# Stage 1 of the first batch in a written order: loads pinned ahead of the projection weights, and products of a zeroed tile at the start

## The chip, the cores and the metric

The kernel runs on one core of a Trainium2 chip. The metric is the device time of the whole program in microseconds (us), as the median of several runs. The engines are TensorE (PE; PEld is its weight load), VectorE (DVE), ScalarE (ACT), GpSimd (POOL) and SyncE (SP), whose queue issues every DMA of this kernel.

## The reference, cut to what matters

Three blocks follow each other, for 2 batches of 768 positions:

- a local attention (8 heads of 64): every position attends to the keys less than 16 away and to 24 block keys, which are the maxima of the keys over blocks of 32; its values are the 48 or 96 values around it and 24 block means. `a = exp(s - max); a / (sum + 1e-9)`, then `a @ v_all`. This is stage 1.
- a layer of 4 experts, each a causal attention (`x @ wq`, `x @ wk`, `x @ wv`, softmax, `a @ v @ wo`), two of them kept for each position by the gate.
- a mixer: `relu(xt @ w_tok1) @ w_tok2` added over the positions, and `relu(u @ w_ch1) @ w_ch2` over the channels, whose weights come as 64-bit floats and are decoded on the chip.

## The kernel before

Stage 1 of one batch works on 4 pairs of heads (hp), each in 3 groups (g) of 4 tiles of 64 queries: 12 groups, numbered 0 to 11. A group goes through these steps:

- `s1_scores` (L205): 4 float32 products of 128x120 into one PSUM bank. One float32 product is two passes in the trace, so a group has 8 rows.
- the minima with the mask (L214, DVE), the exponentials with their sums (L217, ACT), `1e-9` added (L222, POOL), the reciprocal (L223, DVE), the normalization (L225, POOL, one instruction for batch 0);
- `s1_turn` (L233): 4 transposes, copied out by ACT (L235);
- `s1_values` (L244): 8 products (16 passes), copied to x0h by ACT (L248), and the rest of the rounding to x0l by DVE (L249).

Once for a pair of heads, `s1_keys` writes the block maxima into the key tile kx (for the first pair, L170 to L180 also build kx from one plain key tile kt), and `s1_means` makes the block means of batch 0 with 12 products (24 passes, L193), copies them out (ACT, L198) and spreads them into the value tile vx (POOL, L199). Batch 1 sums its means on DVE instead (L186, from the tile vt).

The loads of batch 0 (L156) are kx or kt, the two halves of the queries qb, and vx for each pair; the masks and the identity come with the first. The weights of the projections are loaded by `w_load` (L536, L540: rv and rqk) and split into a high and a low part by `split_w` (L112 on POOL, L113 on DVE, the last quarter on POOL): wv first, then wqk.

The order of the instructions on each engine is found by the framework, which plays the program through with its own costs. What the program text sets is only the order in which `run` draws from its generators. Pinned to the order of the text were the loads of the first two pairs of heads alone (`tc.keep_in_program_order`). `tc.issue_after(x)` puts what a block holds behind `x` on the engine of `x`, with no wait across engines.

Stage 1 of batch 1 and the projections of batch 0 (`proj`: pv, then pj) are drawn together after stage 1 of batch 0. Then come the attention of the experts of batch 0, the projections of batch 1, and the decoding of the mixer's weights (`decode_w`), which stands behind the last x1h on ACT (`gate`).

Of the kernel before, what the change touches and what calls it, by code (L numbers as in the profile page):

```python
# [7 lines left out]
F32 = mybir.dt.float32  # L8
F32R = mybir.dt.float32r
AF = mybir.ActivationFunctionType  # L10
ALU = mybir.AluOpType
# [22 lines left out]
BK = {"sc": 3, "pt": 3, "acc": 2}  # L34
NEGB = -8.0e9
BIG = 3.0e38

F64_TINY = 2.0 ** -15
F64_HUGE = 122880.0
# [3 lines left out]
def stack_kernel(ctx: ExitStack, tc, qT, kT, kwT, vw, vT, wqkv, wo, tok1, tok2, ch1, ch2,  # L43
# [64 lines left out]
        nc.sync.dma_start(raw, src)  # L108
        return raw

    def split_w(hi, lo, r, sub=None):
        gps.tensor_scalar(hi, r, 1.0, 1.0, op0=ALU.mult, op1=ALU.mult)  # L112
        (sub or vec).tensor_sub(lo, r, hi.bitcast(F32))  # L113

    def decode_w(hi, lo, src, n):

# [22 lines left out]
    def s1_load(b, hp, qb):  # L139
        first = b == 0 and hp == 0  # L140
        kx = unit([P, NT, KX], F32, f"kx{b}{hp}")
        kt = None
        if first:

            kt = xunit([P, S + 2 * WIN], F32, "kt")
            vec.memset(kx[:, 0, KW:KX], 0.0)

        vt = half([P, S], F32, "vt") if b else None
        vx = unit([P, NT, P], F32, f"vx{b}{hp}")
        loads = [(kt, kT) if first else (kx, kwT[b, hp])]  # L150
        loads += [(qb[i::2, :, i, :], qT[b, hp, i::2].rearrange("p (t c) -> p t c", c=P)) for i in range(2)]
        if first:
            loads += [(lmask, lmask_d), (ident, ident_d), (blocks, blocks_d)]
        loads += ([(vt, vT[b, hp])] if b else []) + [(vx[:KW], vw[b, hp])]
        for d, src in loads:
            r = nc.sync.dma_start(d, src)  # L156
            if b == 0 and hp < 2:
                tc.keep_in_program_order(r)
        last["load"] = r
        return kt, vt, kx, vx  # L160

# [18 lines left out]
                vec.tensor_copy(*sums)  # L180

    def s1_sums(kt, vt, kx, vx):
        if vt is None:
            return None
        vs = sp1.tile([P, NBLK], F32, name="vs")
        vec.tensor_reduce(vs, vt.rearrange("p (n c) -> p n c", c=BLK), axis=AX.X, op=ALU.add)  # L186
        return vs

    def s1_means(b, hp, vs, vx):
        pv = bank("pt", f"vm{b}{hp}")  # L190
        if vs is None:
            for t in range(NT):
                ten.matmul(pv[:NBLK, :P], blocks[:, 2 * (NT - 1 - t):2 * (NT - 1 - t) + NBLK], vx[:KW, t, :],  # L193
                           start=t == 0, stop=t == NT - 1)
        else:
            ten.transpose(pv[:NBLK, :P], vs, ident)
        vm = sp1.tile([NBLK, P], F32, name="vm")
        act.activation(vm, pv[:NBLK, :P], AF.Copy, scale=1.0 if vs is None else 1.0 / BLK)  # L198
        gps.tensor_scalar(vx[KW:KX], vm[:, None, :].broadcast_to([NBLK, NT, P]), 1.0, 1.0, op0=ALU.mult, op1=ALU.mult)  # L199

    def s1_scores(b, hp, g, qb, kx):
        sc = bank("sc", f"s1s{b}{hp}{g}")
        for i in range(4):
            t = 4 * g + i
            ten.matmul(sc[:, KX * i:KX * i + KX], qb[:, t // 2].rearrange("p i c -> p (i c)")[:, t % 2::2], kx[:, t, :],  # L205
                       start=True, stop=True)
        n = sp1.tile([P, 4, KX], F32, name="n", bufs=2)
        mn = sp1.tile([P, 4], F32, name="mn", bufs=4)
        sm = sp1.tile([P, 4], F32, name="sm", bufs=4)
        pr = sp1.tile([P, 4, KX], F32, name="pr", bufs=3)  # L210
        for i in range(4):
            t = 4 * g + i
            mi = 0 if t == 0 else (2 if t == NT - 1 else 1)
            vec.tensor_tensor_reduce(n[:, i, :], sc[:, KX * i:KX * i + KX], lmask[:, mi, :],  # L214
                                     scale=-0.125, scalar=BIG, op0=ALU.add, op1=ALU.min, accum_out=mn[:, i:i + 1])
        for i in range(4):
# [3 lines left out]
    def s1_norm(b, pr, sm):  # L220
        ri = sp1.tile([P, 4], F32, name="ri", bufs=4)
        gps.tensor_scalar(sm, sm, 1e-9, 1.0, op0=ALU.add, op1=ALU.mult)  # L222
        vec.reciprocal(ri, sm)  # L223
        if b == 0:
            gps.tensor_mul(pr, pr, ri[:, :, None].broadcast_to([P, 4, KX]))  # L225
# [4 lines left out]
    def s1_turn(b, hp, g, pr, sm):  # L230
        pT = bank("pt", f"s1p{b}{hp}{g}")
        for i in range(4):
            ten.transpose(pT[:KX, P * i:P * i + P], pr[:, i, :], ident)  # L233
        pTs = sp1.tile([P, 512], F32, name="pTs", bufs=2)
        act.activation(pTs[:KX], pT[:KX], AF.Copy)  # L235
        return pTs

    def s1_values(b, hp, g, vx, pTs, xh, xl):
# [7 lines left out]
        cs = slice(256 * g, 256 * g + 256)  # L246
        hi, lo = xh[hp // 2][:, hp % 2, cs], xl[hp // 2][:, hp % 2, cs]
        last["x"] = act.activation(hi, av[:, :256], AF.Copy)  # L248
        return lambda: vec.tensor_sub(lo, av[:, :256], hi.bitcast(F32))  # L249

    def s1(b, xh, xl, qbs, lds):

        n = 3 * HP
        nq = len(qbs)
        if lds is None:
            lds = [s1_load(b, 0, qbs[0])]
        st, tr, rest = {}, {}, {}
        s1_keys(*lds[0])
        for i in range(n + 4):
            hp, g = divmod(i, 3)  # L260
            if i < n:
                st[i] = s1_scores(b, hp, g, qbs[hp % nq], lds[hp][2])
                if g == 0 and len(lds) < min(hp + 2, HP):
                    lds.append(s1_load(b, hp + 1, qbs[(hp + 1) % nq]))
            if 0 <= i - 1 < n:
                s1_norm(b, *st[i - 1])
            if i < n:
                if g == 0:
                    vs = s1_sums(*lds[hp])
                if g == 1:  # L270
                    s1_means(b, hp, vs, lds[hp][3])
                    if hp + 1 < HP:
                        s1_keys(*lds[hp + 1])
            if 0 <= i - 2 < n:
                tr[i - 2] = s1_turn(b, *divmod(i - 2, 3), *st[i - 2])
            if i - 4 in rest:
                rest[i - 4]()
            if 0 <= i - 3 < n:
                hp, g = divmod(i - 3, 3)
                rest[i - 3] = s1_values(b, hp, g, lds[hp][3], tr[i - 3], xh, xl)  # L280
            if i < n:
                yield

# [248 lines left out]
    raws = [xunit([P, HP, 260], F32, "rv"), *(xunit([P, HP, 2, P], F32, f"rqk{p}") for p in range(2))]  # L532

    def w_load(i):
        if i == 0:
            nc.sync.dma_start(raws[0], wsrc[:, :, 512:772])  # L536
        else:
            for t in range(2):
                c = 256 * t + P * (i - 1)
                nc.sync.dma_start(raws[i][:, :, t], wsrc[:, :, c:c + P])  # L540
# [20 lines left out]
    g1 = s1(1, *xs[1], qbs[:2], None)  # L561
# [8 lines left out]
    def wt_load():  # L570
        for nm, src, kt_n, n, step in (("t1", tok1, 6, 256, 256), ("t2", tok2, 2, 768, 256), ("wo", wo, 2, 512, 512)):
# [102 lines left out]
```

## Time and profile before

| | us |
|---|---|
| median of 3 runs | 470.71 (470.41 to 471.19) |
| profiled execution, whole time | 472.78 |
| its span, first to last instruction | 470.9 |
| its mean granted clock | 0.992 |
| bytes moved | 46.51 MB |

The page gives the busy share of each engine over the whole span, the span in 40 slices, the chain of work that ended last, and the costliest groups of instructions. A timeline lists instructions in order of time, merged where they follow each other, with the idle time before them in brackets and what ended it. [...]

### The profile page before, as it was taken

How to read it: one execution, taken by the hardware profiler on the slowest of the kernel's cores; microseconds unless marked ns; L12 is line 12 of the kernel's file. 1: busy time of each engine (PE TensorE's matmuls, PEld its weight loads, DVE VectorE, ACT ScalarE, POOL GpSimd, SP SyncE). 2: the span in 40 equal slices, each digit the busy share in tenths (PEclk: the TensorE clock that was granted, in tenths of full speed). 3: DMA queues.
4: the chain of work that ended last, by engine and by line, in shares of the span. 5: the costliest groups of instructions: out<-in, count | busy, mean ns of one | idle time of the engine just before them, and what ended most of it. 6: DMA issues, size and time to landing. Idle time of an engine off the chain costs nothing.

```text
span 470.9 us, 8508 instructions
## 1 busy us (share of the span) xinstructions
PE 445.4 (95%) x3012; PEld 420.4 (89%) x3012; DVE 281.8 (60%) x817; ACT 230.3 (49%) x653; POOL 286.0 (61%) x319
## 2 busy tenths in 40 slices
PE   3998999999989969999999999999999999999996
PEld 3886999889978757888799999999999999999996
DVE  6666665749699759777864643676572673322322
ACT  2666865877778766875764333224324231110110
POOL 5674732758989877898783879877864772000000
PEclk9999999999999997999999999999999999999999
DMA  8999527706515873120211111121221110001111
GB/s 265 289 306 308 150 57 215 170 2 157 134 46 156 202 183 86 46 90 1 89 47 46 45 47 45 46 89 46 89 85 50 47 45 1 0 1 67 68 68 68
DMA packets 28522, 46.51 MB, mean 99 GB/s; under 512 B 2496, under 2 KB 19648, under 8 KB 28480
## 3 DMA queue, kind: packets, MB, share of 16 engines
q1 hardware_dynamic: 28480, 45.97, 34.7%
q8 instruction: 24, 0.39, 0.4%
q14 instruction: 18, 0.15, 0.1%
HBM read 33.38 MB, written 3.15 MB: 78 GB/s over the span
## 4 chain that ended last, share of the span: by engine, by line
PE 70%; DMA 10%; DVE 9%; POOL 5%; issue 3%; ACT 2%; SPq 0%; DVEq 0%; ACTq 0%; POOLq 0%
PE h L102 7%; PE h L103 7%; PE h L101 7%; PE o L101 7%; PE o L102 7%; PE o L103 7%; DMA kx<-in_kwT_dram 5%; PE s1s L205 3%; PE s1a L244 2%; PE u L101 2%; DMA vx<-in_vw_dram 2%; PE u L102 2%; PE u L103 2%; PE s2s L371 2%; PE s2p L397 2%
## 5 line engine op out<-in xcount | busy, mean ns | idle before, releaser
L127 POOL TENSOR_SCALAR deca<-deca 128x512 f32<-128x512 f32 x30 | 57.9, 1934 | 13.4 <-ACT deca L126 12.6
L102 PE MATMUL o<-hl,c2h 128*128 128x384 f32 x192 | 64.2, 337 | 0.0
L103 PE MATMUL o<-hh,c2l 128*128 128x384 f32 x192 | 64.0, 336 | 0.0
L97 ACT ACTIVATE hh<-h 128x384 fp32r<-128x384 f32 x48 | 23.2, 488 | 78.7 <-PE h L103 76.6
L98 DVE SCALAR_TENSOR_TENSOR hl<-h,hh 128x384 fp32r<-128x384 f32 x48 | 26.5, 555 | 53.3 <-ACT hh L97 53.3
L500 DVE TENSOR_TENSOR oa<-o,oa 128x384 f32<-128x384 f32 x64 | 31.9, 549 | 38.3 <-PE o L103 38.3
L101 PE MATMUL o<-hh,c2h 128*128 128x384 f32 x192 | 49.4, 336 | 0.0
L217 ACT ACTIVATE pr<-n,mn 128x120 f32<-128x120 f32 x96 | 36.6, 384 | 22.2 <-DVE mn L214 21.8
L133 POOL TENSOR_TENSOR raw<-raw 128x512 f32<-128x512 f32 x30 | 31.3, 1044 | 21.1 <-DVE raw L130 19.3
L387 POOL TENSOR_SCALAR pr<-pr,f,wg 128x128 f32<-128x128 f32 (+5 forms) x48 | 40.2, 850 | 4.9 <-DVE f L384 1.7
L134 POOL TENSOR_TENSOR deca<-deca,raw 128x512 f32<-128x512 f32 x30 | 40.8, 1359 | 1.0
L132 ACT ACTIVATE raw<-raw 128x512 f32<-128x512 uint32 x30 | 20.3, 677 | 36.5 <-DMA raw<-in_ch_dram 31.5
L128 DVE TENSOR_SCALAR deca<-deca 128x512 int32<-128x512 int32 x30 | 27.5, 918 | 15.2 <-POOL deca L127 15.2
L381 ACT ACTIVATE pr<-pr,mn 128x128 f32<-128x128 f32 (+5 forms) x48 | 32.1, 669 | 9.2 <-DVE mn L376 9.2
L102 PEld LDWEIGHTS o<-hl,c2h 128*128 128x128 f32 x192 | 36.0, 188 | 0.4 <-DVE hl L98 0.3
L103 PEld LDWEIGHTS o<-hh,c2l 128*128 128x128 f32 x192 | 36.0, 188 | 0.0
L205 PE MATMUL s1s<-kx,qb 128*128 128x120 f32 x192 | 28.6, 300 | 7.7 <-DVE wvl L113 7.7
L101 PEld LDWEIGHTS o<-hh,c2h 128*128 128x128 f32 x192 | 34.8, 188 | 0.1
L205 PEld LDWEIGHTS s1s<-kx,qb 128*128 128x128 f32 x192 | 26.6, 212 | 8.2 <-DVE wvl L113 7.7
L102 PE MATMUL h<-u0l,c1h 128*128 128x384 f32 x96 | 32.5, 338 | 0.0
L101 PE MATMUL h<-u0h,c1h 128*128 128x384 f32 x96 | 32.5, 338 | 0.0
L103 PE MATMUL h<-u0h,c1l 128*128 128x384 f32 x96 | 32.3, 337 | 0.0
(202 smaller groups left out, 1327.3 us busy)
## 6 DMA issues: line engine op xcount, KB each, us to landing
raw<-in_ch_dram SPq DMA_DIRECT2D x24, 512.0 KB, 3.6
kx<-in_kwT_dram SPq DMA_DIRECT2D x7, 720.0 KB, 10.2
vx<-in_vw_dram SPq DMA_DIRECT2D x8, 576.0 KB, 9.4
qb<-in_qT_dram SPq DMA_DIRECT2D x16, 192.0 KB, 8.4
raw<-in_tok_dram SPq DMA_DIRECT2D x6, 512.0 KB, 4.5
out_dram<-oa SPq DMA_DIRECT2D x16, 192.0 KB, 2.0
vt<-in_vT_dram SPq DMA_DIRECT2D x4, 384.0 KB, 10.1
rqk<-in_wqkv_dram SPq DMA_DIRECT2D x4, 256.0 KB, 10.3
```

The source lines that it names most:

```text
L101: ten.matmul(out, lh, rh, start=start, stop=False)
L102: ten.matmul(out, lh, rl, start=False, stop=False)
L103: ten.matmul(out, ll, rh, start=False, stop=stop)
L127: gps.tensor_scalar(af, af, F64_TINY, F64_HUGE, op0=ALU.max, op1=ALU.min)
L128: vec.tensor_scalar(ta, ta, 3, 0x3FFFFFFF, op0=ALU.logical_shift_left, op1=ALU.bitwise_and)
L133: gps.tensor_mul(lf, lf, ef)
L134: gps.tensor_add(af, af, lf)
L205: ten.matmul(sc[:, KX * i:KX * i + KX], qb[:, t // 2].rearrange("p i c -> p (i c)")[:, t % 2::2], kx[:, t, :], start=True, stop=True)
L217: act.activation(pr[:, i, :], n[:, i, :], AF.Exp, bias=mn[:, i:i + 1], scale=-1.0, accum_out=sm[:, i:i + 1])
L381: act.activation(prs[r], prs[r], AF.Exp, bias=mn[:, r, ci:ci + 1], scale=-1.0, accum_out=sm[:, r:r + 1])
L387: gps.tensor_scalar(prs[r][:, :nk], prs[r][:, :nk], f[:, r:r + 1], wg[:, 3 * h + r, e:e + 1], op0=ALU.mult, op1=ALU.mult)
L500: vec.tensor_add(oa[d], a[:, :HALF], oa[d])
```

## The change

The steps of stage 1 of batch 0 are taken apart into functions of their own (`s1_minima`, `s1_exps`, `s1_sm`, `s1_ri`, `s1_mul`, `s1_turned`, `s1_high`, `s1_low`), which compute what they did. A new function calls them in the order of a written list, and each instruction that a word of the list traces is tied behind the one traced last on its engine. In the list a word is a step and a group (or a pair of heads): S scores, mn minima, ex exponentials, sm, ri, mu normalization, T transposes, pT their copy, V values, xh and xl the outputs, kx keys, vm a third of the means' products, vme their copy, vx their spreading, wh and wl the split of wv. The words km do nothing. Instructions that are not in the list (the projections, batch 1) may still be placed between them.

```diff
+FIRST = """
+kx0 S0 S1 mn0 ex0 S2 mn1 vm0.0 ex1 sm0 mn2 vm0.1 ri0 km1 mu0 vm0.2 ex2 kx1 sm1 T0 ri1 S3 mu1 pT0 S4
+vme0 sm2 mn3 vx0 ex3 T1 ri2 mn4 S5 mu2 pT1 V0 mn5 ex4 sm3 vm1.0 ri3 km2 mu3 V1 xh0 T2 kx2 sm4 xh1 T3
+xl0 ex5 vm1.1 ri4 xl1 mu4 vm1.2 pT2 sm5 S6 ri5 pT3 mu5 vme1 S7 mn6 vx1 ex6 T4 mn7 T5 S8 km3 ex7 sm6
+V2 ri6 kx3 mu6 V3 mn8 xh2 S9 sm7 pT4 xl2 xh3 ri7 S10 pT5 mu7 mn9 ex8 T6 xl3 T7 V4 ex9 sm8 mn10 V5
+wh0 S11 ri8 wh1 wl0 wh2 pT6 vm2.0 wl1 sm9 wh3 xh4 wl2 mu8 pT7 vm2.1 xl4 ex10 ri9 wl3 vm2.2 mn11 mu9
+T8 vme2 vm3.0 xh5 vx2 ex11 xl5 vm3.1 vm3.2 sm10 ri10 sm11 mu10 ri11 V6 vme3 V7 vx3 pT8 T9 xh6 T10
+xh7 xl6 pT9 mu11 xl7 V8 V9 xh8 pT10 T11 xl8 xh9 V10 pT11 xl9 V11 xh10 xl10 xh11 xl11
+"""
...
         for d, src in loads:
-            r = nc.sync.dma_start(d, src)
-            if b == 0 and hp < 2:
-                tc.keep_in_program_order(r)
+            if b == 0:
+                r = tc.keep_in_program_order(nc.sync.dma_start(d, src))
+            else:
+                with tc.issue_after(last["load"].ins):
+                    r = nc.sync.dma_start(d, src)
         last["load"] = r
...
+    def s1_first(xh, xl, qbs, lds, wsplit):
...
+        for word in FIRST.split():
+            at = len(traced)
+            op = word.rstrip("0123456789.")
+            if op == "vm":
+                block(*map(int, word[2:].split(".")))
+            elif op != "km":
+                step(op, int(word[len(op):]))
+            prev = {}
+            for x in traced[:at]:
+                prev[x.engine] = x
+            for x in traced[at:]:
+                if x.engine in prev:
+                    tc.add_manual_dep(x, prev[x.engine].name, NOSYNC, reason="keep_in_program_order")
+                prev[x.engine] = x
...
+        with tc.issue_after(last["mn", 0, HP - 1, 2].ins):
+            s1_keys(*lds[0])
...
-                if g == 0:
-                    vs = s1_sums(*lds[hp])
-                if g == 1:
-                    s1_means(b, hp, vs, lds[hp][3])
-                    if hp + 1 < HP:
-                        s1_keys(*lds[hp + 1])
+                with tc.issue_after(last["mn", b, hp, 0].ins):
+                    vs = s1_sums(*lds[hp])
+                s1_means(b, hp, vs, lds[hp][3])
+                if hp + 1 < HP:
+                    s1_keys(*lds[hp + 1])
...
+    idle = dec.tile([P, P], F32, tag="raw", name="idle")
+    vec.memset(idle, 0.0)
+    spare = bank("acc", "spare")
+    for i in range(13):
+        tc.keep_in_program_order(ten.matmul(spare[:, :P], idle, idle, start=True, stop=True))
...
     def w_split():
-        for w, r in zip((wv, *wqk), raws):
+        for w, r in zip(wqk, raws[1:]):
             for k in range(HP):
-                split_w(w[0][:, k], w[1][:, k], r[:, k], gps if k == HP - 1 else vec)
+                with tc.issue_after(last["mul"].ins):
+                    split_h(w[0][:, k], r[:, k])
+                    with tc.issue_after(last["mn", 0, HP - 1, 2].ins):
+                        split_l(w[0][:, k], w[1][:, k], r[:, k], gps if k == HP - 1 else vec)
                 yield
...
         lds.append(s1_load(0, hp, qbs[hp]))
-        for i in ((), (0, 1), (2,), ())[hp]:
-            w_load(i)
-    with tc.issue_after(last["load"].ins):
-        nc.sync.dma_start(tri, tri_d)
-        nc.sync.dma_start(cmask, cmask_d)
+    for i in range(3):
+        w_load(i)
+    for t, src in ((tri, tri_d), (cmask, cmask_d)):
+        last["load"] = tc.keep_in_program_order(nc.sync.dma_start(t, src))
+    head = last["load"]
...
-    run((12, s1(0, *xs[0], qbs, lds)), (3 * HP, w_split(), 0.3, 1))
+    s1_first(*xs[0], qbs, lds, [
...
-    run((12, g1), (18, part(p0, 10)))
+    run((12, g1), (18, part(p0, 10)), (2 * HP, w_split(), 0, 0.3))
...
-                    with tc.issue_after(gate.ins):
+                    with tc.issue_after(gate.ins), tc.issue_after(head.ins):
```

`w_load` pins its loads as well. So the SP queue begins with all loads of batch 0, then rv, the four rqk, tri and cmask; the loads of batch 1 and of the mixer's weights follow. The buffer of kt is taken one place earlier among the units it shares with rv and rqk.

## Rows read from the trace of the kernel before

**Rows 1.** The page, part 1: busy time, share of the span, instructions of each engine.
```profile
PE 445.4 (95%) x3012; PEld 420.4 (89%) x3012; DVE 281.8 (60%) x817; ACT 230.3 (49%) x653; POOL 286.0 (61%) x319
```

**Rows 2.** Windows: busy time of each engine, clock, DMA share, GB/s.
```profile
5.00:10.00 5.00, 2.27 (x11) 2.31 (x11) 3.67 (x11) 0.00 (x0) 2.65 (x5) 1.00 1.11 301
10.00:15.00 5.00, 5.00 (x35) 4.77 (x35) 3.75 (x28) 4.18 (x21) 1.38 (x3) 1.00 1.07 307
47.00:105.00 58.00, 57.98 (x599) 53.30 (x598) 34.70 (x195) 42.41 (x172) 30.88 (x73) 1.00 0.48 121
120.00:200.00 80.00, 70.95 (x427) 61.59 (x426) 63.47 (x189) 59.88 (x156) 68.29 (x70) 0.96 0.47 119
```

**Rows 3.** Timeline of PE: start, us, instruction, count, idle before and its releaser.
```profile
7.73 5.22 PE L205 MATMUL s1s<-kx,qb 128*128 128x120 f32 x24 [7.73 <-DVE wvl L113]
12.87 2.80 PE L193 MATMUL vm<-vx,blocks 96*24 96x128 f32 x24
...
33.72 0.65 PE L233 MATMUL s1p<-ident,pr 128*120 128x128 f32 x4 [0.24 <-POOL pr L225]
...
37.80 0.54 PE L233 MATMUL s1p<-ident,pr 128*120 128x128 f32 x3 [0.59 <-POOL pr L225]
...
41.57 0.69 PE L244 MATMUL s1a<-pTs,vx 120*64 120x64 f32 x16 [0.93 <-ACT pr L217]
...
45.09 0.69 PE L244 MATMUL s1a<-pTs,vx 120*64 120x64 f32 x16 [0.84 <-DVE ri L223]
```

**Rows 4.** The chain that ended last, 0 to 130: start, us, what.
```profile
2.25 4.71 DMA qb<-in_qT_dram
...
16.80 11.49 DMA kx<-in_kwT_dram
...
46.68 0.44 PE s1p L233 x4
47.11 0.94 PE s1s L205 x8
...
49.97 0.61 PE s1a L244 x16
```

**Rows 5.** Windows to 45.71 of L205, L193, L233 and L244, in this order.
```profile
0.00:45.71 45.71, 14.24 (x91) 13.30 (x91) 1.00 1.02 290
...
0.00:45.71 45.71, 11.57 (x96) 9.40 (x96) 1.00 1.02 290
...
0.00:45.71 45.71, 5.98 (x36) 3.86 (x36) 1.00 1.02 290
...
0.00:45.71 45.71, 5.85 (x128) 4.60 (x128) 1.00 1.02 290
```

**Rows 6.** Timelines of DVE and POOL: start, first keys, first normalization.
```profile
0.95 1.51 DVE L524 MEMSET qb<- 128x768 f32 x2 [0.95 <-PEq L663]
...
3.72 0.95 DVE L170 TENSOR_REDUCE km<-kt 128x24 f32<-128x768 f32 x1 [1.23 <-DMA kt<-in_kT_dram]
...
6.00 0.51 DVE L180 COPY kx<-km 128x288 f32<-128x288 f32 x1
...
12.58 0.99 POOL L225 TENSOR_TENSOR pr<-pr,ri 128x480 f32<-128x480 f32 x1 [0.55 <-DVE ri L223]
```

**Rows 7.** Groups by line, 7.7 to 47: count, busy us, mean ns, idle before.
```profile
L217 ACT ACTIVATE pr<-n,mn 128x120 f32<-128x120 f32 x44 | 16.8, 382 | 18.6 <-DVE mn L214 18.5
...
L113 DVE TENSOR_TENSOR wqk0l<-rqk,wqk0h 128x256 fp32r<-128x256 f32 x3 | 2.0, 694 | 1.6 <-POOL wqk0h L112 1.6
...
L112 POOL TENSOR_SCALAR wqk0h<-rqk 128x256 fp32r<-128x256 f32 x4 | 1.8, 460 | 1.5 <-DMA rqk<-in_wqkv_dram 1.4
```

**Rows 8.** Timeline of POOL: the first decoding instruction.
```profile
104.36 3.82 POOL L127 TENSOR_SCALAR deca<-deca 128x512 f32<-128x512 f32 x2 [4.27 <-ACT deca L126]
```

**Rows 9.** Waits of the SP queue, and its issue of batch 1's last keys.
```profile
SPq L344 <- ACT s000h L93: 16.8, 1, 16.8
...
74.88 0.77 SPq L156 DMA_DIRECT2D kx<-in_kwT_dram  x1
```

More of the change, by code (lines that the diff above doesn't have):

```diff
@@ L190, in s1_means @@
         pv = bank("pt", f"vm{b}{hp}")
[L191 to L196, printed above, removed]
+        ten.transpose(pv[:NBLK, :P], vs, ident)
         vm = sp1.tile([NBLK, P], F32, name="vm")
-        act.activation(vm, pv[:NBLK, :P], AF.Copy, scale=1.0 if vs is None else 1.0 / BLK)
+        act.activation(vm, pv[:NBLK, :P], AF.Copy, scale=1.0 / BLK)
         gps.tensor_scalar(vx[KW:KX], vm[:, None, :].broadcast_to([NBLK, NT, P]), 1.0, 1.0, op0=ALU.mult, op1=ALU.mult)
@@ L206, in s1_scores, with s1_minima, s1_exps @@
                        start=True, stop=True)
+        return sc
+    def s1_minima(b, hp, g, sc):
         n = sp1.tile([P, 4, KX], F32, name="n", bufs=2)
         mn = sp1.tile([P, 4], F32, name="mn", bufs=4)
+        for i in range(4):
+            t = 4 * g + i
+            mi = 0 if t == 0 else (2 if t == NT - 1 else 1)
+            last["mn", b, hp, g] = vec.tensor_tensor_reduce(
+                n[:, i, :], sc[:, KX * i:KX * i + KX], lmask[:, mi, :],
+                scale=-0.125, scalar=BIG, op0=ALU.add, op1=ALU.min, accum_out=mn[:, i:i + 1])
+        return n, mn
+    def s1_exps(n, mn):
         sm = sp1.tile([P, 4], F32, name="sm", bufs=4)
@@ L211, in s1_scores, with s1_sm, s1_ri, s1_mul @@
         for i in range(4):
[L212 to L216, printed above, removed]
             act.activation(pr[:, i, :], n[:, i, :], AF.Exp, bias=mn[:, i:i + 1], scale=-1.0, accum_out=sm[:, i:i + 1])
         return pr, sm
-    def s1_norm(b, pr, sm):
+    def s1_sm(sm):
+        gps.tensor_scalar(sm, sm, 1e-9, 1.0, op0=ALU.add, op1=ALU.mult)
+    def s1_ri(sm):
         ri = sp1.tile([P, 4], F32, name="ri", bufs=4)
-        gps.tensor_scalar(sm, sm, 1e-9, 1.0, op0=ALU.add, op1=ALU.mult)
         vec.reciprocal(ri, sm)
+        return ri
+    def s1_mul(b, pr, ri):
         if b == 0:
-            gps.tensor_mul(pr, pr, ri[:, :, None].broadcast_to([P, 4, KX]))
+            last["mul"] = gps.tensor_mul(pr, pr, ri[:, :, None].broadcast_to([P, 4, KX]))
         else:
@@ L233, in s1_turn, with s1_turned @@
             ten.transpose(pT[:KX, P * i:P * i + P], pr[:, i, :], ident)
+        return pT
+    def s1_turned(pT):
         pTs = sp1.tile([P, 512], F32, name="pTs", bufs=2)
@@ L245, in s1_values, with s1_out, s1_high @@
                            pTs[:KX, P * i + 64 * j:P * i + 64 * j + 64], start=True, stop=True)
[L246 to L251, printed above, removed]
+        return av
+    def s1_out(hp, g, x):
+        return x[hp // 2][:, hp % 2, 256 * g:256 * g + 256]
+    def s1_high(hp, g, av, xh):
+        last["x"] = act.activation(s1_out(hp, g, xh), av[:, :256], AF.Copy)
@@ new lines, in s1_low, with block, mean, step @@
+    def s1_low(hp, g, av, xh, xl):
+        vec.tensor_sub(s1_out(hp, g, xl), av[:, :256], s1_out(hp, g, xh).bitcast(F32))
+    def s1_first(xh, xl, qbs, lds, wsplit):
+        box = {}
+        def block(hp, p):
+            if p == 0:
+                box["vm", hp] = bank("pt", f"vm0{hp}")
+            pv, vx = box["vm", hp], lds[hp][3]
+            for t in range(4 * p, 4 * p + 4):
+                ten.matmul(pv[:NBLK, :P], blocks[:, 2 * (NT - 1 - t):2 * (NT - 1 - t) + NBLK], vx[:KW, t, :],
+                           start=t == 0, stop=t == NT - 1)
+        def mean(hp):
+            box["vme", hp] = sp1.tile([NBLK, P], F32, name="vm")
+            act.activation(box["vme", hp], box["vm", hp][:NBLK, :P], AF.Copy)
+        def step(op, i):
+            hp, g = divmod(i, 3)
+            if op == "S":
+                box["S", i] = s1_scores(0, hp, g, qbs[hp], lds[hp][2])
+            elif op == "mn":
+                box["mn", i] = s1_minima(0, hp, g, box["S", i])
+            elif op == "ex":
+                box["ex", i] = s1_exps(*box["mn", i])
+            elif op == "sm":
+                s1_sm(box["ex", i][1])
+            elif op == "ri":
+                box["ri", i] = s1_ri(box["ex", i][1])
+            elif op == "mu":
+                s1_mul(0, box["ex", i][0], box["ri", i])
+            elif op == "T":
+                box["T", i] = s1_turn(0, hp, g, box["ex", i][0])
+            elif op == "pT":
+                box["pT", i] = s1_turned(box["T", i])
+            elif op == "V":
+                box["V", i] = s1_values(0, hp, g, lds[hp][3], box["pT", i])
+            elif op == "xh":
+                s1_high(hp, g, box["V", i], xh)
+            elif op == "xl":
+                s1_low(hp, g, box["V", i], xh, xl)
+            elif op == "kx":
+                s1_keys(*lds[i])
+            elif op == "vme":
+                mean(i)
+            elif op == "vx":
+                gps.tensor_scalar(lds[i][3][KW:KX], box["vme", i][:, None, :].broadcast_to([NBLK, NT, P]), 1.0, 1.0,
+                                  op0=ALU.mult, op1=ALU.mult)
+            elif op == "wh":
+                wsplit[i][0]()
+            elif op == "wl":
+                wsplit[i][1]()
+        traced = nc.cur_bb.bb.instructions
+        for word in FIRST.split():
[12 more added lines that the diff above has]
+                prev[x.engine] = x
@@ L253, in s1 @@
+    def s1(xh, xl, qbs):
+        b = 1
         n = 3 * HP
         nq = len(qbs)
[L255 to L258, printed above, removed]
+        lds = [s1_load(b, 0, qbs[0])]
+        ex, pTs, av = {}, {}, {}
+        with tc.issue_after(last["mn", 0, HP - 1, 2].ins):
+            s1_keys(*lds[0])
         for i in range(n + 4):
@@ L530, in stack_kernel @@
     wsrc = wqkv.rearrange("(k p) n -> p k n", p=P)
-    raws = [xunit([P, HP, 260], F32, "rv"), *(xunit([P, HP, 2, P], F32, f"rqk{p}") for p in range(2))]
+    raws = [xunit([P, HP, 260], F32, "rv"), xunit([P, HP, 2, P], F32, "rqk0")]
+    kt0 = xunit([P, S + 2 * WIN], F32, "kt")
+    raws.append(xunit([P, HP, 2, P], F32, "rqk1"))
     def w_load(i):
         if i == 0:
-            nc.sync.dma_start(raws[0], wsrc[:, :, 512:772])
+            tc.keep_in_program_order(nc.sync.dma_start(raws[0], wsrc[:, :, 512:772]))
         else:
```

41 lines of the change are left out of this document (25 added, 16 removed).

## The prediction

> **What bounds the kernel now.** I read the page's engine shares first: TensorE is busy 95% of the span [rows 1], so time can be gained where it stands still or works slowly, and only if the engines behind it follow. Then the windows [rows 2]. From 47 to 105 us TensorE is busy 57.98 of 58.00 us while no other engine reaches 43: there the end moves with the amount of TensorE work still to be done. From 120 to 200 us it is busy 70.95 of 80.00, with POOL at 68.29 and DVE at 63.47. The waste that this change can reach lies before 47 us. The PE timeline [rows 3] shows it as three things: nothing runs until 7.73; the first 24 passes of scores take from 7.73 to 12.87, 0.214 us each, where eight of the same passes take 0.94 us, 0.1175 each, once the stage runs [rows 4]; and between 33 and 45 us there are waits of 0.24, 0.59, 0.93 and 0.84 us for the softmax of this stage.
>
> [...]
>
> **The sum, step by step.** The work of stage 1 of batch 0 on TensorE at full pace, by passes: 96 of scores at 0.1175 (0.94/8), 48 transposes at 0.11 (0.44/4), 192 of values at 0.038 (0.61/16) [rows 4], 96 of means at 0.117 (2.80/24) [rows 3]: 11.3 + 5.3 + 7.3 + 11.2 = 35.1 us.
>
> Before: by 45.71 the trace has 91, 36, 128 and 96 of these [rows 5], worth 10.7 + 4.0 + 4.9 + 11.2 = 30.8 us, in the 37.98 us since 7.73. So 7.2 us were lost: 5.14 - 24 x 0.1175 = 2.3 to the slow pace, 2.6 to the four waits, and the remaining 2.3 to small gaps at changes from one kind of product to another. What is missing is worth 35.1 - 30.8 = 4.3 us. Had TensorE done only this work, it would have ended at 50.0.
>
> After, the start. The zeroed tile needs one DVE instruction at its start, which before was at 0.95 us [rows 6]; a memset six times as large took 0.75 us, so TensorE can begin at about 1.3. 13 float32 products of 128 columns are 26 passes; no row shows one, so I scale the slow scores' pass by 128/120: 0.228 us, 5.9 us for all. They end at about 7.2 if all are slow, and at about 6.6 if the last five run at full pace, as scores did after 5.1 us of work. S0 waits for nothing longer: the keys of the first pair were built by 6.51 [rows 6], and the queries, which landed at 6.96 with rv and one rqk ahead of them [rows 4], now have only kt ahead. I take 6.9 for the start of S0, at full pace.
>
> [...]
>
> After, the written order. I followed each engine through the list with the durations of the trace. T0 has to wait for mn0, ex0, sm0, ri0 and mu0; before, that took from 9.43 (S0's end) to 13.57 [rows 6], 4.1 us. The list puts S1, S2 and vm0 there, 2 x 0.94 + 2.8 = 4.7 us of TensorE. Later each T has at least five TensorE words between it and its scores. ACT has the next largest load, an exponential of a tile every 0.38 us [rows 7], 18.3 us for 48, under 31 with its copies, against 35.1 of TensorE. With in-order engines I find no wait of TensorE over 0.2 us. The pinned order has a price: a late load stands in front of everything behind it on DVE (kx1 before ri1, kx3 before mn8). By the shapes in the code kt is 400 KiB, the queries of a pair 384, the masks 261, vx 576, kx 720. kt landed at 3.7 [rows 6], and from there on some 300 GB/s flowed, 293 KiB/us [rows 2]. Before, that puts the fourth pair's kx, the 7,245th KiB with rv and rqk ahead, at 3.7 + 6,845/293 = 27.1; it landed at 28.3 [rows 4], 1.2 late. In the new order kx1 is the 2,341st KiB, at 10.3, or 11.5 if as late, needed at 11 to 12; kx3 the 5,701st, at 21.8 to 23, needed at 24.5. So 0 to 1 us is lost there, and I take 0.3. The small gaps need not vanish: at the rate of before they are 2.6 us; the list puts longer runs of one kind together, so I take half, 1.3 (0 to 2.6).
>
> Together: 6.9 + 35.1 + 0.3 + 1.3 = 43.6 against 50.0, a gain of 6.4 us. At best 6.6 + 35.1 = 41.7, a gain of 8.3. At worst 7.2 + 35.1 + 1 + 2.6 + 2.3 (scores slow again) = 48.2, a gain of 1.8.
>
> **What is moved.** The loads of rv, rqk, tri and cmask, some 1.8 MiB or 6 us of DMA, fall behind the other loads of batch 0. rv, the 7,181st KiB, lands at about 27 and is first needed at wh0, behind mu7, at about 28; rqk lands at about 30. SP's queue otherwise issues the same loads, and batch 1's first pair (2,064 KiB more) lands by 38 to 40, before TensorE asks for it at 43: nothing. Without this cover the first projection would wait up to 3 us. The splits of wqk fall behind mu11 on POOL and mn11 on DVE: 8 x 0.46 + 2 x about 0.7 = 5.1 us of POOL and 6 x 0.69 = 4.2 of DVE [rows 7], issued from about 40 us on instead of from 17.7. They meet a POOL that is busy 30.88 of 58 us between 47 and 105 [rows 2], and pj asks for them only after some 9 us of pv and the first groups of batch 1. Nothing; without cover up to 5.1 us. Batch 1's keys and sums get edges behind the minima on DVE, which have run by then.
>
> **The rest of the program.** From 47 to 105 us TensorE has no gap [rows 2], so a lead at 44 us should be a lead at 105. There POOL takes over: its decoding starts at 104.36, when ACT released it [rows 8], and ACT's part stands behind the last x1h. It moves with the lead. But the order of everything behind stage 1 is found anew. TensorE idles 9.05 us between 120 and 200 [rows 2]; I let a third of that go either way, 3 us, and take 0.
>
> So the span goes from 470.9 to 464.5, and the whole profiled execution from 472.78 to 466.4. The profiled execution lies 2.07 us above the median of 470.71; taken from the median, the gain gives **464.3 us**.
>
> **Rivals.**
>
> - *The zeroed products do not raise the pace* (the clock follows something that zeros don't supply, or rises late): S0 to S2 are slow again, 464.3 + 2.3 = 466.6. For it: only real scores were ever seen to raise it. Against: TensorE was just as occupied. Chance 0.13.
> - *Loads late by about 3 us* at S3, S6 or S9, with DVE and TensorE standing behind one another: 464.3 + 3 = 467.3. For it: the fourth keys took 11.5 us from issue to landing [rows 4], and kx1 has under a microsecond of slack. Against: rv and rqk no longer stand ahead. Chance 0.05.
> - *The gain is given back between 105 and 200 us*: POOL and DVE set the pace there, and in a new order TensorE idles 15 us instead of 9: 464.3 + 6.4 = 470.7, 469 to 473 around it. For it: 68 of 80 us of POOL. Against: POOL's own start moves with x1h. Chance 0.11.
> - *Slower: batch 1's keys behind the queries' copies on SP.* SP stood 16.8 us for s000h, and the keys of the fourth pair were issued only behind that, at 74.88 [rows 9]. If the new order puts the third pair's loads there too, TensorE loses a landing, some 10 us, and about 1.3 us of key work, less what else it has. With all of pj for the second half still to do (48 passes, 8.4 us) it is hidden; from the point where that is already done, it costs 11 us: 475. Chance 0.11.
>
> Forecast as reckoned 0.60, range 461 to 467.5. Less than 0.2% (0.94 us) is what a measurement of this kernel cannot tell from no change. Forecast, first and second rival are faster (0.78); of the third 0.02 is faster, 0.07 the same, 0.02 slower; the fourth is slower. Faster 0.80, same 0.07, slower 0.13. The range 461 to 471 leaves out the fourth rival, the upper part of the third and about 0.05 below.
>
> **What would show it right or wrong.** Right: TensorE busy from about 1.3 us; S0 at 6.6 to 7.2 with eight passes in about 0.94 us; no wait over 0.3 us until V11, which ends at 42 to 45; pv right behind; the first decoding on POOL at about 98; 57 to 58 us busy of any 58 in between. Wrong by a step: eight scores in 1.7 us (first rival); DVE waiting for kx before ri1 or mn8 (second); the decoding at 98 but the idle time between 115 and 195 at 15 us (third); a wait of TensorE between 45 and 100 us with a kx issued behind k or q copies (fourth). The prediction as a whole is wrong if V11 ends before 45 and the time is not under 468.

## The result: 1% faster, inside the forecast, though two of its terms were far off

The changed kernel takes 466.52 us (median of 9 runs, 464.61 to 469.34), the kernel before in the same session 471.19 (469.62 to 475.14). The ratio is 0.9895, with a 95% interval of 0.9857 to 0.9933: a gain of about 5 us (4.7 by the medians) where 6.4 were forecast. The profiled execution took 467.73 us with a span of 465.9, against 472.78 and 470.9. Medians and ranges, here and below, are over all executions; the ratios leave out the few that are over 1.5% above the fastest of their kernel.

The timeline of PE after the change, with the columns of [rows 3], shows the start and the first surprise:

```profile
1.04 5.87 PE L630 MATMUL spare<-idle 128*128 128x128 f32 x26 [1.04 <-DVE idle L627]
6.74 2.98 PE L217 MATMUL s1s<-kx,qb 128*128 128x120 f32 x24
11.37 2.78 PE L293 MATMUL vm<-vx,blocks 96*24 96x128 f32 x24 [1.66 <-DMA vx<-in_vw_dram]
14.08 0.65 PE L257 MATMUL s1p<-ident,pr 128*120 128x128 f32 x4
15.93 2.12 PE L217 MATMUL s1s<-kx,qb 128*128 128x120 f32 x16 [1.20 <-DMA qb<-in_qT_dram]
...
48.23 0.50 PE L217 MATMUL s1s<-kx,qb 128*128 128x120 f32 x2 [2.29 <-DVE mn L227]
...
54.02 0.73 PE L217 MATMUL s1s<-kx,qb 128*128 128x120 f32 x4 [0.36 <-DVE mn L227]
54.91 1.15 PE L271 MATMUL s1a<-pTs,vx 120*64 120x64 f32 x32
```

The zeroed products run from 1.04, and the 24 passes of S0 to S2 behind them take 2.98 us, 0.124 each, where they took 5.22 [rows 3]. Then TensorE waits 1.66 us for vx0 and 1.20 for the queries of the second pair. From there to 48.23 the timeline shows no wait at all: the four waits for the softmax of [rows 3] are gone. At 48.23 and 54.02 it waits 2.29 and 0.36 us for minima of batch 1, and the last values of batch 0 end only at 56.06.

What held those minima up stands in the timeline of DVE and in its waits up to 60 us (engine, line waited for: us, times, longest):

```profile
DVE km L185 <- DMA kx<-in_kwT_dram: 10.5, 3, 5.8
```
```profile
46.41 0.95 DVE L185 TENSOR_REDUCE km<-kx 128x24 f32<-128x768 f32 x1 [5.82 <-DMA kx<-in_kwT_dram]
47.28 0.27 DVE L227 CUSTOM_DVE_ANT_0 n<-s1s,lmask 128x120 f32<-128x120 f32 x1
...
49.17 0.75 DVE L282 TENSOR_TENSOR x0l<-s1a,x0h 128x256 fp32r<-128x256 f32 x2
```

The block maxima of batch 1's second pair of keys (L185) stood on DVE for 5.82 us until their kx had landed. The minima for scores that were already there, and the lows of x0, were queued behind it.

The windows answer to [rows 2] (47 to 105: 57.98 busy before; the last three numbers of a row are TensorE's granted clock as a share of its full speed, the DMA share and GB/s), and POOL's first decoding to [rows 8] (104.36 before):

```profile
47.00:105.00 58.00, 55.46 (x578) 51.13 (x579) 38.84 (x199) 42.06 (x165) 30.19 (x73) 1.00 0.55 143
```
```profile
103.06 3.82 POOL L144 TENSOR_SCALAR deca<-deca 128x512 f32<-128x512 f32 x2 [3.35 <-ACT deca L143]
```

So of the lead only 1.3 us is left at the first decoding. The other 3.7 of this pair's 5.0 us came later: 366.5 us passed from there to the end of the span before, 362.8 after. The place is the same step in both traces, before and then after:

```profile
176.99 1.65 PE L402 MATMUL s2a<-pf,V 128*128 128x384 f32 x2 [3.87 <-ACT pf L401]
```
```profile
173.16 0.91 PE L507 MATMUL s2a<-pf,V 128*128 128x384 f32 x2 [1.31 <-ACT pf L506]
```

Before, ACT stood behind a tile of channel weights whose load took from 166.47 to 173.95 (7.48 us in the chain of waits); TensorE then waited 3.87 us instead of 1.31, and its granted clock was 0.64 from 175 to 180 and 0.84 from 180 to 190, against 1.00 after. How much of this belongs to the change is what a second profile can tell.

### The profile page after: what moved, and what is told of

It reads as the page before. It is cut to its first block, busy times and chain, and to the rows that moved or that the text cites. A ratio compares the mean times of both kernels' runs of the same rounds, so it can differ in the third digit from the quotient of the medians.

```text
span 465.9 us, 8565 instructions
## 1 busy us (share of the span) xinstructions
PE 445.1 (96%) x3038; PEld 420.7 (90%) x3038; DVE 280.1 (60%) x818; ACT 231.2 (50%) x653; POOL 285.2 (61%) x319
## 4 chain that ended last, share of the span: by engine, by line
PE 68%; DMA 10%; DVE 7%; POOL 4%; ACT 3%; issue 3%; SPq 3%; DVEq 0%; ACTq 0%; POOLq 0%
PE h L113 7%; PE h L112 7%; PE h L114 7%; PE o L112 7%; PE o L113 7%; PE o L114 7%; DMA kx<-in_kwT_dram 5%; PE s1s L217 4%; PE s1a L271 2%; DMA qb<-in_qT_dram 2%; POOL pr L492 2%; PE u L112 2%; PE pj L112 2%; PE u L113 2%; PE u L114 2%
## 5 line engine op out<-in xcount | busy, mean ns | idle before, releaser
L112 PE MATMUL h<-u1h,c1h 128*128 128x384 f32 x96 | 32.3, 336 | 0.0
L113 PE MATMUL h<-u1l,c1h 128*128 128x384 f32 x96 | 32.3, 336 | 0.0
## 6 DMA issues: line engine op xcount, KB each, us to landing
vx<-in_vw_dram SPq DMA_DIRECT2D x8, 576.0 KB, 11.1
```

What stands on the lines that cost most here:

```text
L112: ten.matmul(out, lh, rh, start=start, stop=False)
L113: ten.matmul(out, lh, rl, start=False, stop=False)
```

## The experiments

Ratios are those to the kernel before on the same chip, with their 95% intervals.

**A second profile of both kernels, unedited.**

> The kernel before, unchanged, profiled once more. Theory A (chance): in the first trace TensorE stood 3.87 us from 173 to 177 behind ACT, which waited 2.61 us for the second raw tile of the channel weights (7.5 us to landing); the order there is the same as in the changed kernel, where that tile came without a wait. If that is chance, this look shows that wait at some other length, most likely under 1 us, and TensorE's idle time from 120 to 200 us differs from 9.05 by 2 us or more. Rival B (cause): the wait belongs to the kernel before; it stands here again at 2 us or more. In both, the stretch up to 105 us repeats: S0 at 7.7, slow scores until 12.9, the first decoding on POOL at 104.4 within 0.4 us.

> The changed kernel, unchanged, profiled and timed again beside the kernel before. Theory A (chance after 165 us): the first decoding on POOL again at 103.1 within 0.4 us, 1.3 us ahead of the kernel before; what is gained beyond that differs from execution to execution, and the median gain of the pairs comes out between 1.5 and 5 us. Rival B (the gain is made behind 165 us by the change itself): TensorE's idle time from 120 to 200 us is again 7.7 us or less while the second look at the kernel before has 9 or more, and the median gain is 4.7 us within 1.

Before: one run of 472.22, span 470.3, first decoding at 105.77. After: 467.13 (465.67 to 468.13, 6 runs), ratio 0.9883 (0.9852 to 0.9913), span 465.1, first decoding at 102.47. This time the lead at the decoding is 3.3 us and what follows gives 1.9 (364.5 against 362.6): the split moves between executions, the gain of about 5 does not. That both decodings would repeat within 0.4 us was wrong: the kernel before came 1.4 us later, the changed one 0.6 sooner.

Theory A does not hold. In the second profile of the kernel before, TensorE waits at the same step again, 2.49 us where theory A had under 1 and rival B 2 or more; the granted clock was 0.91 from 165 to 180 (1.00 in the second profile after the change), and the idle time from 120 to 200 was 7.97 us, 1.08 less than in the first and not 2.

```profile
176.97 1.37 PE L402 MATMUL s2a<-pf,V 128*128 128x384 f32 x2 [2.49 <-ACT pf L401]
```

After the change this wait was 1.31 us in both profiles. The start of the changed kernel repeated in part: vx0 was late again, and the wait for batch 1's keys was 5.88 us. What differed, on the timeline of PE:

```profile
6.23 2.98 PE L217 MATMUL s1s<-kx,qb 128*128 128x120 f32 x24
10.85 3.75 PE L293 MATMUL vm<-vx,blocks 96*24 96x128 f32 x24 [1.64 <-DMA vx<-in_vw_dram]
14.53 1.11 PE L257 MATMUL s1p<-ident,pr 128*120 128x128 f32 x4
```

After a wait of 1.64 us the granted clock from 10.85 to 14.60 was 0.72, and the means took 3.75 us instead of 2.78; after the 1.66 us of the first profile it stayed at 1.00. Two waits of the same length, then, and one of them was followed by about 1 us more for the means; why that one is not shown. The second pair's queries were not waited for this time, so that the slow means cost nothing in the end: S3 began at 15.43, against 15.93.

**Batch 1's later keys behind the last low of x0 on DVE.**

```
 def s1_low(...):
-    vec.tensor_sub(...)
+    last["low"] = vec.tensor_sub(...)
 ...                                   # in s1, batch 1
+        low0 = last["low"]
 ...
-                s1_keys(*lds[hp + 1])
+                with tc.issue_after(low0.ins):
+                    s1_keys(*lds[hp + 1])
```

> The changed kernel with one edge more: the keys of batch 1's second pair stand behind the last x0l on DVE. Theory (a late load stands in front on DVE): the keys waited 5.8 us for their load at 46.4, and minima of batch 1 and the x0l of the groups 6 and 7 stood behind them; TensorE lost 2.3 us at 48.2 and 0.4 at 54.0. Without that block it loses under 0.5 there, the first decoding on POOL comes at 100.4 to 101 instead of 103.1, and the time is 1.5 to 3 us under the changed kernel's. Rival 1 (DVE is only the last of several): TensorE then waits for the second pair's scores themselves, and the gain is under 0.7 us. Rival 2: the keys come too late for batch 1's second pair and cost 1 us or more.

> A second look at the kernel keys_late, whose profiled run was its fastest (465.85) with 470.56 in the median. Theory (its executions differ in how soon the first loads land): if this run is above 468, it shows waits of 2 us or more together for vx0 and the second pair's queries before 18 us, and S9 or T10 waits for DVE or POOL behind them, while 47 to 105 stays busy over 57 of 58. Rival (the edge on the keys): the waits before 18 us are as in its first profile (under 1.9 us), and the time is lost between 45 and 105 us at the keys.

470.56 us (465.85 to 474.74, 12 runs), ratio 0.9955 (0.9921 to 0.9989). The edge does what it says, the waits at 48 and 54 us are gone; yet the kernel is slower than the changed one of the same session (0.9883, and the intervals do not overlap). The profiled run was its fastest, and one in which vx0 came without a wait and the second queries 0.71 us late. The second profiled run, of 469.38 and on another chip, had them late:

```profile
11.62 2.78 PE L293 MATMUL vm<-vx,blocks 96*24 96x128 f32 x24 [1.85 <-DMA vx<-in_vw_dram]
...
15.93 2.12 PE L217 MATMUL s1s<-kx,qb 128*128 128x120 f32 x16 [0.95 <-DMA qb<-in_qT_dram]
...
62.21 0.69 PE L271 MATMUL s1a<-pTs,vx 120*64 120x64 f32 x16 [1.50 <-DVE lg L407]
81.56 0.73 PE L217 MATMUL s1s<-kx,qb 128*128 128x120 f32 x4 [0.65 <-DVE kx L187]
```

Both theories hold in part. The loads explain 1.9 of the 3.5 us between the two runs (S3 began at 15.93 against 14.00), and S9 waited another 0.37 us for minima. Then come waits that the changed kernel does not have: TensorE stands behind a copy on DVE at 62 us and for the keys at 81 (0.28 and 0.16 us in the faster run). In front of that copy stood the block maxima of the third pair, 2.96 us until their kx had landed (1.73 in the faster run).

**No zeroed products.**

```
-    for i in range(13):
-        tc.keep_in_program_order(ten.matmul(spare[:, :P], idle, idle, start=True, stop=True))
```

> The changed kernel without the 13 products of the zeroed tile. Theory L (loads set the pace of the first 16 us): scores take 5.1 us from 6.7 at the latest, so the first means start at about 11.9 instead of 11.4, but the second pair's scores wait for their queries until 15.9 in both; the first decoding on POOL stays at 103.1 within 0.5, and the time is that of the changed kernel within 0.7 us. Rival P (the pace of the scores counts): everything from the means on is 2.3 us later, the decoding at 105.4, and the time 2.3 us higher.

470.2 us (466.43 to 475.59, 9 runs), ratio 0.9925 (0.989 to 0.996), against 0.9883 with them. They are worth about 2 us here by the ratios and 3 by the medians, about what the slow scores cost; the intervals overlap, so the size is rough. It speaks against theory L, which had that time hidden behind the late loads (within 0.7 us). Where the 2 us go is not shown: the profiled execution took 475.59, far above the median.

**The parts one at a time.** The written order and the products with the loads issued as before:

```
-            if b == 0:
-                r = tc.keep_in_program_order(nc.sync.dma_start(d, src))
-            else: ...
+            r = nc.sync.dma_start(d, src)
+            if b == 0 and hp < 2:
+                tc.keep_in_program_order(r)
 ...
+        for i in ((), (0, 1), (2,), ())[hp]:
+            w_load(i)
 ...
```

> The changed kernel with the loads issued as before the change: rv and one half of rqk ahead of the first queries, the rest of rqk and the masks between the later pairs; order and zeroed products stay. Theory (pinning the loads bought little at the start, because vx0 and the second pair's kx and queries landed no earlier than before): S0 at about 7.0, vm0 and S3 wait together 1.5 to 4 us as now (2.86); the loads of the third and fourth pair land as before (kx3 at about 28 against the written order's need at 24.5), so S9 waits a further 2 to 4 us. Batch 1's loads are no later than now. Time 469 to 470.5, 2 to 3.5 us above the changed kernel. Rival (the loads' place does not matter at all, what counts is how fast they flow): 466.5 to 468, S9 without a wait over 0.5 us.

468.88 us (466.2 to 472.55, 12 runs), ratio 0.9951 (0.9922 to 0.998), a shade under the theory's range and outside the rival's. The start was better than the theory had it: S0 began at 7.71, after 1.25 us for its queries, and vm0 and S3 waited only 0.47 together, although rv and a part of rqk were ahead of their loads again. But S9 waited 3.39 us for minima that stood behind a later pair's keys, as the theory said:

```profile
31.72 2.62 PE L215 MATMUL s1s<-kx,qb 128*128 128x120 f32 x16 [3.39 <-DVE mn L225]
```

The same without the products (both edits together):

> The written order alone: loads as before the change, no zeroed products. order_old_loads (with the products) measured 468.9 and a ratio of 0.9951. Theory (the order makes the products pay, which alone brought nothing): S0 to S2 slow from 7.0 to 12.4, the values' means 1.3 us later than with the products, S9 waits less because it comes later while its keys land at the same time; 469.5 to 471, ratio 0.997 to 1.000. Rival (order and products just add up, products at nothing): ratio 0.995 as order_old_loads.

470.42 us (468.84 to 476.43, 12 runs), ratio 0.9949 (0.9917 to 0.9981). The ratio is the rival's: with the loads of before, the products bring nothing to the written order that shows beyond the intervals of 0.3%. S0 to S2 took 5.29 us, S9 then waited only 0.48, and at 44.10 TensorE waited 2.73 us for batch 1's keys, for which DVE had stood 5.55: the loads set the pace either way.

The kernel before with the products alone, and with the new loads alone:

> The kernel before with the 13 zeroed products alone. Theory (the products raise TensorE's pace by themselves; they are worth what the slow scores cost, as far as the means' operand allows): the 24 passes of S0 to S2 take 2.8 us instead of 5.14, from 7.7 to 10.5; then the means wait for vx0, which landed at about 11.1, so 0.6 us of the 2.3 is lost again and 1.7 us is left at 15 us; the softmax of the stage gives some of it back by its waits for ACT and DVE, and 0.5 to 1.7 us remain at the end: 469.5 to 471.5 beside a kernel before of 470.7 to 472.7, ratio 0.996 to 0.999. Rival (a lead at the start of the old order is given back in full, because the late fourth pair at 28 us and the softmax set its pace): S9 and the values behind it at the same instants as before, ratio 0.999 to 1.001.

> The kernel before with its loads alone in the new order (all loads of batch 0 ahead of rv, rqk and the masks), no zeroed products, the planner's own order of stage 1. Theory (the loads are worth little without the written order): the fourth pair's kx lands at about 22 to 24 instead of 28.3, S0 starts 0.5 to 1 us sooner but slow; the waits of TensorE between 33 and 45 us (2.6 us before) fall by 1 us at most, as they are for the softmax; rv lands at 27 to 28 and its splits, which the planner puts among the steps of stage 1, hold DVE and POOL: 470 to 473, ratio 0.995 to 1.003. Rival (late loads were the real limit of the stage before): the waits vanish, a lead of 3 us or more at 45 us, ratio under 0.993.

Products: 471.87 us (469.17 to 478.86, 12 runs), ratio 0.999 (0.9953 to 1.0028): no change that can be told from noise, though the upper part of the theory's range is not excluded. The scores ran fast (3.06 us), the means then waited 0.60 us for vx0, and between 41 and 49 us the old order waited for POOL and ACT as before. Loads: 474.58 us (473.22 to 477.5, 9 runs), ratio 1.0072 (1.0043 to 1.0102), slower than the theory allowed. This order of loads, alone, costs 3.4 us; the timeline of PE shows vx0 late and, here, the second pair's keys:

```profile
6.16 5.34 PE L207 MATMUL s1s<-kx,qb 128*128 128x120 f32 x24 [6.16 <-DVE kx L182]
12.02 2.78 PE L195 MATMUL vm<-vx,blocks 96*24 96x128 f32 x24 [0.52 <-DMA vx<-in_vw_dram]
16.79 0.97 PE L207 MATMUL s1s<-kx,qb 128*128 128x120 f32 x6 [1.99 <-DVE kx L170]
```

With S0 1.57 us sooner than before, these two waits are not the whole cost; the rest is not separated.

**vx0 issued second, in SP's empty 0.7 us.** After the change SP issues kt at 0.72 and then nothing until 1.88, since the queries' tile is being zeroed by DVE; before, rv and rqk stood in that gap. The timeline of SP after the change:

```profile
0.72 0.39 SPq L174 DMA_DIRECT2D kt<-in_kT_dram  x1
1.88 1.43 SPq L174 DMA_DIRECT2D qb<-in_qT_dram  x2
```

The edit puts one load there that is needed early:

```
+        if first:
+            loads.insert(1, loads.pop())
         for d, src in loads:
```

> The changed kernel with the first value tile vx0 issued second, right behind kt, in the 0.7 us in which SP otherwise stands for the memset of the queries' tile. Theory (the stall of 2.86 us comes from SP's late start of the loads: 0.7 us without an issue and vx0 issued at 4.95): vx0 lands by 8.5 instead of 11.3, the means' products wait for nothing, S0 starts by 7.2, the second pair's queries land about 0.7 us sooner, at 15.2, and S3 waits about 2.2 us: total stall to S3 2.2 instead of 2.86, V11 0.7 us sooner, the time 0.5 to 1 us under the changed kernel (466 to 466.6), with the wait on DVE for batch 1's keys unchanged. Rival (the transfer engines are full from 3 us on, so that what is put first pushes back what follows): kt or the first queries land 1.5 to 2 us later, S0 at 8 to 9 and slow or not, no gain or 1 us slower (467 to 468.5).

463.38 us (463.06 to 465.5, 5 runs), ratio 0.9838 (0.9811 to 0.9864): the fastest kernel of this study, 2.1 to 2.7 us better than the changed kernel by the ratios (of different sessions). The theory's mechanism is right and its size too small; S0 came later than it said, as the rival had it in kind (7.61, after 0.93 us for the queries), and everything behind it sooner. Its timeline of PE:

```profile
7.61 3.06 PE L219 MATMUL s1s<-kx,qb 128*128 128x120 f32 x24 [0.93 <-DMA qb<-in_qT_dram]
10.59 2.80 PE L295 MATMUL vm<-vx,blocks 96*24 96x128 f32 x24
13.33 0.65 PE L259 MATMUL s1p<-ident,pr 128*120 128x128 f32 x4
13.81 2.04 PE L219 MATMUL s1s<-kx,qb 128*128 128x120 f32 x16
...
44.78 0.49 PE L219 MATMUL s1s<-kx,qb 128*128 128x120 f32 x2 [1.03 <-DVE mn L229]
```

The windows say why, of the changed kernel and of this one (the last two numbers are DMA share and GB/s):

```profile
3.00:4.00 1.00, 1.00 (x7) 1.00 (x7) 0.32 (x1) 0.00 (x0) 1.00 (x2) 1.00 0.42 128
5.00:10.00 5.00, 4.71 (x34) 4.53 (x32) 3.03 (x24) 1.80 (x9) 0.10 (x1) 1.00 0.92 258
10.00:15.00 5.00, 3.36 (x28) 2.81 (x28) 2.20 (x12) 3.07 (x17) 1.28 (x3) 1.00 1.06 274
```
```profile
3.00:4.00 1.00, 1.00 (x7) 1.00 (x7) 0.00 (x0) 0.00 (x0) 1.00 (x2) 1.00 1.10 381
5.00:10.00 5.00, 4.07 (x30) 3.91 (x29) 2.42 (x19) 0.85 (x5) 0.00 (x0) 1.00 1.07 325
10.00:15.00 5.00, 5.00 (x45) 4.54 (x44) 3.08 (x21) 4.54 (x23) 2.64 (x6) 1.00 1.04 316
```

With the gap the DMA engines moved 128 GB/s from 3 to 4 us and 258 to 274 after it; with vx0 in the gap 381, 325 and 316. Before the change these were 349, 301 and 307 (the last two in [rows 2]). Other profiles bear this out. With the gap, in both profiles of the changed kernel, in the first with the keys' edge and in that without the products, it was 90 to 143 GB/s from 3 to 4 us and 219 to 272 from 5 to 10; with rv and rqk or vx0 in the gap, in the first profile of the kernel before, in that with the loads of before and in that with vx0 second, 349 to 381 and 291 to 325. In these seven it is the gap, and not which load fills it, that goes with the rate. Neither vx0 nor the second queries are waited for any more, and the first decoding comes at 98.32. On DVE batch 1's second keys, still waited for, are there 3.8 us sooner (46.41 in the changed kernel):

```profile
42.62 0.95 DVE L187 TENSOR_REDUCE km<-kx 128x24 f32<-128x768 f32 x1 [4.22 <-DMA kx<-in_kwT_dram]
```

**The same with the keys' edge, and the same without the products** (the edits shown above, combined).

> vx0 second in SP's order as in vx_first, and the keys of batch 1's later pairs behind the last x0l on DVE as in keys_late. Theory (with the loads in time, what is left of the wait on DVE for batch 1's second keys is 1.0 us before S and 0.2 before V; the edge takes it away, and the spread of keys_late came from its loads): no wait of TensorE over 0.3 us between 15 and 105, first decoding on POOL at about 97.2, 462 to 463.2, 0.3 to 1.3 us under vx_first. Rival (the edge itself costs, because the keys are built later and the second pair's scores are missed when TensorE has used up pv): 465 to 468 with runs far apart as in keys_late (465.9 to 474.7), and a wait of TensorE for the keys between 47 and 105.

> vx_first without the 13 zeroed products. Theory (with the loads in time nothing hides the slow scores): S0 to S2 take 5.1 to 5.3 us instead of 3.06, V11 comes 1.2 to 2.3 us later (S0 itself would start at the same 7.6 us, when the queries land), 464.6 to 465.7. Rival P (without them the clock is late again further on, as the low stretches of no_products showed, 0.66 at 35 to 40 us): 466.5 or more. Rival L (something else than TensorE sets the pace of the stage, so the products bring nothing): 463.4 as vx_first.

With the edge: 465.55 us (463.91 to 468.0, 6 runs), ratio 0.9854 (0.981 to 0.9898). The theory falls: the wait of 1.03 us is gone, but the values at 59.68 wait 1.24 us for a copy on DVE and scores at 78.76 wait 0.37 for the keys. Loads in time don't make the edge pay; it moves the wait, to behind the third pair's keys (2.69 us on DVE at 58.31). The profiled run was the slowest of the six, at 468.0. Without the products: 466.04 us (464.69 to 467.52, 6 runs), ratio 0.9863 (0.9823 to 0.9903); S0 to S2 took 5.45 us from 7.57, and the first decoding came at 100.08, 1.8 us later. By the ratios the products are worth 1.2 us here, by the medians 2.1 (5.80 against 7.93 under the kernel before of each session), a size that the intervals don't settle.

## Why the forecast was right, and where it was not

**The start and the pace: right.** S0 began at 6.74 (6.9 said, 6.6 to 7.2 as the sign), and its passes took 0.124 us, not 0.214 [rows 3]. The 2.3 us that the worst case added for scores slow again are shown by no run with the products: S0 to S2 took 2.98 to 3.06 us in all eight profiles with them, and 5.22 to 5.45 in the profiles of five kernels without. The first rival, zeros that don't raise the pace, is refuted, and removing the products cost about 2 us, near the 2.3 at which the slow pace was priced.

**The written order: right.** No wait over 0.2 us was forecast apart from loads; from 17.9 to 48.2 there is none. T0, with the words of the list in front of it, did not wait.

**"0 to 1 us is lost there, and I take 0.3": mis-sized, 2.86.** This is the second rival's amount (about 3, with a chance of 0.05), at S3 but also at vm0. I followed the keys through the queue by a rate of 293 KiB per us, and never asked it of vx0 or the second queries. vx0 had landed at about 11.1 before the change as well (issued at 5.31, landed 5.8 us later); with the slow scores nobody noticed, as the means started at 12.87 [rows 3]. Making S0 to S2 faster brought the means to it. And the rate was that of before, when rv and rqk filled SP's first gap: taking them out of the front left the gap, and the rate fell to 258. With vx0 in the gap 2.86 us of waits became none, though S0 itself began 0.9 us later. For the second queries this shows the gap as the cause, as the same loads are ahead of them. For vx0 that edit alone does not, since it moves vx0 forward too; but with the loads of before, and more of them ahead, vx0 was there at 11.09, not later than the 11.37 of the changed kernel.

**"Nothing" for batch 1's loads: mis-sized, 2.65.** I priced what TensorE would ask for, by the landing of the first pair at 38 to 40. It was the second pair that mattered, and the queue where it was waited for was DVE's: there the block maxima of its keys stood in front of minima and lows that were ready. The prediction had followed the written order's queue for late keys ("kx1 before ri1, kx3 before mn8") and not gone on into batch 1, whose order the planner makes.

With these two, the prediction's sum comes to 6.4 + 0.16 for S0 - 2.56 - 2.65 = 1.35 us, against 1.30 at the first decoding (98 was said, 103.06 measured). That it fits so closely is chance. A further wait for minima, 0.95 us at 64.64, where the third pair's keys stood on DVE for 1.49 us, belongs to the same error and takes the sum to 0.40; what makes up for it is not separated. In the second pair the lead was 3.3 us with waits of much the same size. Two of the prediction's signs failed with it: TensorE was busy 55.46 of the 58 us from 47 to 105, not 57 to 58, and it waited more than 0.3 us before V11. That V11 did not end at 42 to 45 but at 56.06 is no loss by itself: batch 1's scores and pv stand between the values (in the faster kernel it ended at 52.04).

**"The rest of the program 0 ± 3": +3.7 in the profiled pair, +1.9 in the second.** From the first decoding to the end of the span, four profiles with the old order show 363.5 to 366.5 us, and seven with the written order and without the edge on the keys 362.6 to 363.8. So the rest was mostly shorter in the written order, by 1.3 us between the medians, and the 366.5 of the profiled kernel before is the longest of all. The late tile of weights has a part in that (3.87 us of waiting against 1.31), and the longer wait is not one execution's chance: in all six profiles without the zeroed products, of either order, TensorE waited 2.02 to 3.87 us at this step, and in all eight with them 0.88 to 1.32. In the first pair the tile took 7.48 us to land before, and after the change at most 4.6. The zeroed tile is taken from the same two buffers (`tag="raw"`) as these tiles; that this shifts them is a possible cause that no run tests. Nor does the wait alone set the length of the rest: with vx0 first and no products it was 2.02, and the rest 362.7. Three profiles with the edge have 364.6 to 366.0; why stays open. The third rival, a gain given back there, did not happen, nor the fourth: only the last pair's keys were issued behind the queries' copies, at 74.45 (74.88 in [rows 9]), and no wait of TensorE followed up to 105.

So the time fell inside the range with a lead that was 3 to 5 us too large and a rest that was 2 to 4 better than reckoned: in part by luck. The 466.52 us is nearer to the second rival's 467.3 than to the 464.3 forecast, and the first rival's 466.6 fits it as well; only the traces tell them apart. What supports the sum is the kernel with vx0 first: where vx0 and the second queries are in time, the first decoding comes 6.0 us before that of [rows 8], near the 6.4 that were forecast, and the ratio of 0.9838 is 7.6 us.

**How the parts add up.** They don't: alone the products bring nothing that shows (0.999), the loads cost 0.7%, the order gains 0.5%; order and products 0.5%, order and loads 0.75%, all three 1.1 to 1.2%, with vx0 moved 1.6%. Steps of 0.3% or less are within the intervals. The products paid only beside the pinned loads (about 2 us, late loads or not); with the loads of before, S9 gave back in the written order what the start had gained (3.39 us of waiting against 0.48). The pinned loads cost 3.4 us in the old order and gained 2.6 to 3.2 in the written one with the products.

## What to carry to other kernels

When a stage's start is made faster, ask of each operand behind it when it lands, also of those that nobody waited for: slack that the slow start gave is gone with it (here 1.66 us of waiting for vx0). A load that is moved back from the front of a queue leaves its issue slot (0.7 us of SP here), and the slot belongs to whatever is needed first and waits for nothing. An engine's queue, in which one late load can hold what is ready behind it (5.82 us on DVE here), has to be followed past the end of the part that was written out by hand, to the first instruction there that waits for a transfer. And a difference far behind the change is looked for in every profile at hand before it is called chance.

## What was not expected of the hardware

0.7 us without an issue at the start cost more than 0.7 us of transfer: 128 GB/s for a microsecond, and then 258 instead of 325 for five, and 90 to 143, then 219 to 272, in the four profiles with this gap named above. Why the rate stays lower after the gap is open; the mix of the transfers differs too.

Executions of one kernel differ in when its first loads land: in two profiles of the kernel with the keys' edge, on two chips, vx0 was waited for 1.85 us (469.38 in all) and not at all (465.85). The chip alone does not explain it: the changed kernel, with the same loads up to there, waited 1.64 us for vx0 on the chip of the run that did not wait.
